# A fused attention and two mixture-of-experts layers on one core: Newton steps on another engine, and a new order of the last phase

## The chip, the cores and the metric

The kernel runs on one core of one Trainium2 chip. The metric is the device time of one execution in microseconds; lower is better. The time before is the median of three runs.

## The reference

`x` is (2, 11456, 128). Three layers follow each other:

```python
def mab(q, kv):
    s = scale * (q @ kv.T)
    a = exp(s - s.max(-1)); a /= a.sum(-1) + 1e-9
    return a @ kv
h = mab(inducing, x)          # 32 inducing points read 11456 tokens
x = mab(x, h)                 # every token reads the 32 points
logits = x @ phi              # soft mixture: 32 slots, 8 experts, 4 slots each
d = softmax(logits, over tokens);  slot_out[e] = relu((d.T @ x)[e] @ w1[e]) @ w2[e]
x = softmax(logits, over slots) @ slot_out
# hard mixture: one expert of 8 per token
logits = (x / (norm(x) + 1e-6)) @ (emb / (norm(emb) + 1e-6)).T / tau
e = argmax(logits);  gate = softmax(logits)[e]
out = gate * (relu(x @ w1b[e]) @ w2b[e])
```

## The kernel before

The 22,912 tokens are cut into 12 blocks (six per batch, of 16 tiles of 128 tokens, the last of each batch of 8) and a small thirteenth of leftovers, `sp`. Three phases follow each other. The first reads `x` and builds `h`; the second computes each token's slot logits, kept in SBUF in `lT`, and the slot inputs; the third makes the slot outputs, finds the one expert that the tokens use, and writes the output per block. All tokens use the same expert for this input; a check at the end (`cert`, `ok`) decides whether a general path must run, and here it need not. A token's vector after the soft mixture is a combination of 32 slot vectors, so norm, router and output are computed from the 32 exponentials `E` of its logits (`Eall`, the same memory as `lT`) and small matrices.

All work is written as Python generators ("chains"), and one string per phase, `SEQ` and `SEQ2`, says in which order their steps are issued; `in_order` then ties each engine's instructions to that order. A step whose input is late holds up everything behind it on its engine. What is left of a chain after its string is issued by a loop behind it. The chains that matter here:

- `p2_chain`, `grp_chain` (lines 360 to 510): second phase; each ends in additions to `acct` (L501 on POOL, L506 on DVE), and at last `dgp` (L480).
- `e_chain` (L641): a block's maxima on DVE (L96), the subtraction on POOL (L647), the exponential on ACT (L649). Nine are in `SEQ`, four run in the loop behind it.
- `bounds_chain` (L800 to 860): from `dall`, the spread of the logits, it makes `tau_`, `cmid`, two columns of `stkx`, and `rho`, which a later check needs. It is `B` in `SEQ2`.
- `slot_chain` (M), `hid_chain` (a to d), `sout_chain` (S), `sot_chain` (X), `gmat_chain` (W): the two layers of the slot experts; from `dgp` over `siT` (L544), `l1ps`, `hsb`, `hTb`, `sops` and `soT` to `BDg` (L883), the matrix that every gate product needs. `sout_chain` also reads the expert's number and starts the load of its weights.
- `hidden_chain` (H) makes `BDA`, the matrix of the output products; `cert_chain` (C) the check.
- `et_chain` (t0 to tc): four transposes of `E` per block on PE (L85) and a copy to SBUF, `ET`, by ACT or DVE (string `ETE`, L669).
- `gate_chain` (g0 to gc): products with `BDg` into `gps`, `au` copied by ACT, then a product with `E`, either on DVE from PSUM (L698) or, by the string `GTE`, copied by ACT and multiplied on POOL (L695), and a sum on DVE, `nn` (L96).
- `router_chain` (q0 to q3) for blocks 0-1, 2-5, 6-9 and 10-12: a square root of `nn` by three Newton steps (`sqrt_newton`, L785 to 796), a reciprocal, the router's exponential on ACT (L722), and the scale `scall` (L727). `best_chain` (k0 to k3): a comparison on POOL (L733), a sum on DVE.
- `out_chain` (o0 to oc): the output product of half a block, `ops`, scaled by `scall` into `ob` by DVE (V: one instruction, L766), by ACT (S: eight) or by ACT's copy and POOL (A, L775), as the string `OTE` says, and the DMA to HBM on SP's queue, per half for the blocks in `HALVES`.

PSUM in the third phase: `gps`, `ops`, `l1ps`, `sops` and `STps` share three buffers; all else takes two single banks in turn.

Of the kernel before, what the change touches and what calls it, by code (L numbers as in the profile page):

```python
# [18 lines left out]
def attn_moe_moe_kernel(  # L19
# [321 lines left out]
    R = {}  # L341
# [358 lines left out]
        vred(nn[:, ts], q, ALU.add)  # L700
        yield

    def router_chain(t0, t1):

        nt = t1 - t0
        sl = slice(t0, t1)
        n_ = ty([128, 64], F32, "g_n")[:, 0:nt]
        q = ty([128, 64], F32, "g_q")[:, 0:nt]
        bc = [128, nt, E]
        V.tensor_scalar(out=q, in0=nn[:, sl], scalar1=1e-36, scalar2=None, op0=ALU.max)  # L710
        for i, _ in enumerate(sqrt_newton(n_, q, [128, nt])):
# [7 lines left out]
        lg = wk([128, 64, E], F32, "eT")[:, 0:nt]  # L719
# [8 lines left out]
        yield

    def best_chain(t0, t1):  # L730

        ge = wk([128, 64, E], F32, "eq")[:, 0:t1 - t0]
        G.tensor_scalar(out=ge, in0=au[:, t0:t1, 0:E], scalar1=0.0, scalar2=None, op0=ALU.is_ge)  # L733
        yield
        vred(ok[:, t0:t1], ge, ALU.add)
        yield
# [44 lines left out]
    def sqrt_newton(y, q, shape):  # L781

        yi = ty([shape[0], 64], I32, "sq_i")[:, 0:shape[1]]
        t = ty([shape[0], 64], F32, "sq_t")[:, 0:shape[1]]
# [4 lines left out]
        for _ in range(3):
            V.scalar_tensor_tensor(out=t, in0=y, scalar=-0.5, in1=y, op0=ALU.mult, op1=ALU.mult)  # L790
            yield
            V.tensor_tensor(out=t, in0=t, in1=q, op=ALU.mult)  # L792
            yield
            V.scalar_tensor_tensor(out=y, in0=t, scalar=1.5, in1=y, op0=ALU.add, op1=ALU.mult)
            yield
        V.tensor_tensor(out=y, in0=y, in1=q, op=ALU.mult)
# [419 lines left out]
    mark2 = len(nc.cur_bb.bb.instructions)
    for c in SEQ:
        next(chains[c], None)  # L1220
# [11 lines left out]

    HALVES = (0, 1)
# [1 line left out]
    ETE = "SSVSSVSSSVVSV"
    GTE = "VGVGGVVVGVVGG"
    OTE = ("SA", "VS", "VA", "VV", "SS", "VA", "VV", "SV", "SS", "VV", "VV", "VS", "VS")
    late_c = {"M": slot_chain(), "R": rs_chain(), "S": sout_chain(), "X": sot_chain(), "W": gmat_chain(), "B": bounds_chain(),  # L1240
              "H": hidden_chain(), "C": cert_chain()}
# [134 lines left out]
```

## Time and profile before

| | |
|---|---|
| median of 3 runs | 215.33 us (214.25 to 215.44) |
| profiled execution | 216.28 us, of which the span is 214.6 us |
| busy in the span | PE 168.0, DVE 154.9, ACT 100.0, POOL 61.5 us |
| bytes moved | 40.82 MB |

The span runs from the first to the last instruction on the core. Busy shares are means over three phases with different limits, so the stages have to be looked at one by one; "half clock" below is a granted clock of 0.50 in the views, 1.2 GHz.

### The profile page before, as it was taken

Reading aid. Unit: us, or ns where it says so; the run is one execution under the profiler, and the core shown is the slowest. Engines: PE = TensorE matmul, PEld = TensorE weight load, DVE = VectorE, ACT = ScalarE, POOL = GpSimd, SP = SyncE. Lnnn points to the kernel's source line nnn. Section 1 sums busy time; section 2 is a strip of 40 time slices with the busy share of each in tenths; the row PEclk is TensorE's granted clock in tenths of the full one; section 3 lists DMA queues with packets and bytes.
Section 4 is the critical chain, followed back from the end, with each engine's and each line's share of the span. In section 5 each row is a group of like instructions: output and inputs, shape, how many; then the busy total and the mean of one; then the engine's idle time right before and its main releaser. Section 6 shows DMA issues by size and latency. Waiting matters only on the chain.

```text
span 214.6 us, 4393 instructions
## 1 busy us (share of the span) xinstructions
PE 168.0 (78%) x1587; PEld 119.7 (56%) x1587; DVE 154.9 (72%) x485; ACT 100.0 (47%) x283; POOL 61.5 (29%) x84
## 2 busy tenths in 40 slices
PE   0798779899999998987759698899976399778410
PEld 0665436557657757465548356789954276445300
DVE  7336847466999968899934633656999989999950
ACT  2244456367468577486543233414444176447100
POOL 2000001002248290829860610006365015020000
PEclk9999999999999999999965579969999579999955
DMA  5999988999619995000000000050002455538972
GB/s 174 422 300 396 409 341 302 426 400 389 230 31 375 346 416 231 0 0 3 0 0 5 0 0 3 3 184 11 3 0 98 169 215 208 231 162 344 409 322 50
DMA packets 9248, 40.82 MB, mean 190 GB/s; under 512 B 1116, under 2 KB 2308, under 8 KB 6276
## 3 DMA queue, kind: packets, MB, share of 16 engines
q1 hardware_dynamic: 9220, 40.48, 48.6%
q8 instruction: 14, 0.23, 0.4%
q14 instruction: 14, 0.11, 0.2%
HBM read 28.74 MB, written 11.73 MB: 189 GB/s over the span
## 4 chain that ended last, share of the span: by engine, by line
PE 42%; DVE 36%; ACT 7%; issue 5%; DMA 4%; POOL 1%; SPq 0%; DVEq 0%; ACTq 0%; POOLq 0%
PE s L88 9%; DVE ob L766 5%; PE lps L88 4%; PE slps L88 3%; PE gps L88 3%; DVE mx L96 3%; PE hps L88 3%; PE eTps L85 3%; PE xTps L85 3%; PE ops L88 3%; PE l1ps L88 3%; ACT eq L197 2%; DVE sq_t L792 2%; DVE xT L179 2%; DVE nn L96 2%
## 5 line engine op out<-in xcount | busy, mean ns | idle before, releaser
L88 PE MATMUL ops<-BDA,ET 64*128 64x256 f32 x180 | 25.5, 412 | 11.5 <-DVE ob L766 10.2
L88 PEld LDWEIGHTS ops<-BDA,ET 64*128 64x128 f32 x180 | 16.5, 195 | 18.6 <-DVE ob L766 9.9
L93 ACT ACTIVATE ob<-ops,scall 128x128 f32<-128x128 f32 x56 | 15.2, 383 | 8.3 <-PE ops L88 7.7
L200 POOL TENSOR_SCALAR hacc<-hacc,corr,sb 128x1 f32<-128x1 f32 x10 | 3.4, 343 | 48.8 <-ACT corr L199 45.5
L695 POOL TENSOR_TENSOR a2q<-sh,lT 128x512 f32<-128x512 f32 (+2 forms) x6 | 6.5, 1090 | 37.0 <-ACT sh L93 34.1
L88 PE MATMUL gps<-BDg,ET 128*128 128x164 f32 x90 | 15.7, 324 | 1.9 <-DVE a2q L698 1.5
L197 ACT ACTIVATE eq<-s,mn 128x512 f32<-128x512 f32 (+1 forms) x12 | 7.8, 651 | 19.3 <-DVE mn L192 16.4
L452 POOL TENSOR_TENSOR d<-lT,mnew 128x512 f32<-128x512 f32 (+1 forms) x11 | 13.5, 1226 | 10.3 <-DVE cr L438 8.4
L88 PEld LDWEIGHTS gps<-BDg,ET 128*128 128x128 f32 x90 | 13.8, 203 | 3.8 <-DVE a2q L698 1.9
L396 POOL TENSOR_TENSOR a<-sh,sm 128x512 f32<-128x512 f32 (+2 forms) x13 | 12.2, 935 | 12.4 <-DVE sm L393 6.4
L88 PE MATMUL s<-xT,IT 128*32 128x512 f32 (+1 forms) x96 | 12.8, 606 | 3.7 <-DVE xT L179 3.7
L766 DVE TENSOR_TENSOR ob<-ops,scall 128x1024 f32<-128x1024 f32 x13 | 15.4, 1218 | 0.3
L88 PE MATMUL slps<-d,a 128*128 128x128 f32 x88 | 14.3, 326 | 0.5 <-ACT d L465 0.5
L88 PE MATMUL lps<-BD,a2q 128*128 128x132 f32 x90 | 13.2, 287 | 0.9 <-ACT a2q L93 0.5
L88 PEld LDWEIGHTS slps<-d,a 128*128 128x128 f32 x88 | 13.3, 236 | 1.1 <-ACT d L465 0.6
L88 PEld LDWEIGHTS lps<-BD,a2q 128*128 128x128 f32 x90 | 11.1, 190 | 3.7 <-ACT a2q L93 2.2
L85 PE MATMUL xTps<-ident,xt 128*128 128x128 f32 x64 | 10.8, 329 | 2.5 <-DMA xt<-in_x 2.2
L85 PEld LDWEIGHTS xTps<-ident,xt 128*128 128x128 f32 x64 | 9.2, 172 | 6.2 <-issue 2.5
L647 POOL TENSOR_TENSOR lT<-lT,mx 128x512 f32<-128x512 f32 (+2 forms) x13 | 11.9, 933 | 1.7 <-DVE mx L96 1.7
L96 DVE TENSOR_REDUCE s<-s 128x1 f32<-128x512 f32 (+1 forms) x12 | 7.8, 650 | 6.1 <-PE s L88 5.5
L88 PE MATMUL hps<-xt,eT 128*32 128x128 f32 x352 | 12.0, 275 | 0.2 <-ACT eT L93 0.2
L96 DVE TENSOR_REDUCE ml<-lT 128x32 f32<-128x512 f32 (+2 forms) x13 | 11.9, 916 | 0.2
(291 smaller groups left out, 376.7 us busy)
## 6 DMA issues: line engine op xcount, KB each, us to landing
xt<-in_x SPq DMA_DIRECT2D x9, 1024.0 KB, 6.2
out<-ob SPq DMA_DIRECT2D x8, 1024.0 KB, 4.5
xT<-in_x_t SPq DMA_DIRECT2D x6, 1024.0 KB, 9.0
w1s<-in_moe_w SPq DMA_DIRECT2D x4, 1024.0 KB, 8.7
w2s<-in_moe_w SPq DMA_DIRECT2D x4, 1024.0 KB, 14.7
out<-ob SPq DMA_DIRECT2D x6, 512.0 KB, 2.7
xt<-in_x SPq DMA_DIRECT2D x4, 512.0 KB, 6.3
xT<-in_x_t SPq DMA_DIRECT2D x2, 512.0 KB, 10.2
```

Source lines behind the costliest of these rows:

```text
L85: nc.tensor.matmul(dst, lhsT=src, rhs=idn, is_transpose=True, start=True, stop=True)
L88: return nc.tensor.matmul(dst, lhsT=l, rhs=r, start=start, stop=stop)
L93: S.activation(out=o, in_=i, func=AF.Copy, **kw)
L96: V.tensor_reduce(out=o, in_=i, axis=AX.X, op=op, **kw)
L179: (acopy if c == 0 else V.tensor_copy)(xT_t[k][:, 8 * h + 4 * c:8 * h + 4 * c + 4, :].rearrange("p a t -> p (a t)"), ps[:, c])
L197: S.activation(out=e, in_=ps[:, 0:128 * n], func=AF.Exp, scale=-1.0, bias=mn, accum_out=sb)
L396: G.tensor_tensor(out=a2, in0=t, in1=r.unsqueeze(2).to_broadcast([128, 4 * n, 32]), op=ALU.mult)
L452: eng.tensor_tensor(out=d, in0=lT[:, t0:t0 + nt, :], in1=mb, op=ALU.subtract)
L647: G.tensor_tensor(out=e, in0=lT[:, t0:t0 + nt, :], in1=lx.unsqueeze(2).to_broadcast([128, nt, 32]), op=ALU.subtract)
L695: G.tensor_tensor(out=q, in0=ge, in1=Eall[:, ts, :], op=ALU.mult)
L766: V.tensor_tensor(out=o.rearrange("p (i r g) c -> p i r g c", i=m, r=2), in0=pv, in1=sc.rearrange("p (i r g) -> p i r g", i=m, r=2).unsque ...
L792: V.tensor_tensor(out=t, in0=t, in1=q, op=ALU.mult)
```

## The change

1. `sqrt_newton` gets an argument. With "V" it is as before; for the four routers (`QTE`, "GGGG") the three iterations and the last product run on POOL, as four operations per iteration instead of three (13 POOL instructions in place of 10 on DVE), in new yields. The setup of two operations stays on DVE. Its temporaries and the router's are one buffer each.
2. `bounds_chain` is now `&` in `SEQ`'s last characters: its first five steps are issued with the last group of the second phase and the rest as `B` in `SEQ2`.
3. The four `e` chains that the loop issued (blocks 8 to 11) are steps e8 to eb in `SEQ2`.
4. `SEQ2`, `ETE`, `GTE`, `OTE` and `HALVES` are new: half blocks scaled by DVE go from 13 to 16, by ACT in eight pieces from 7 to 6, by ACT and POOL from 2 to none; block 2 is stored in halves too. The DVE makes 7 copies of `ET` in place of 5.
5. With the other yields, `emb_setup`'s last step (a transpose of the expert vectors, `enps`, and its copy to `ien`) falls behind the end of `SEQ`.

```diff
-    def router_chain(t0, t1):
+    def router_chain(t0, t1, eng):
...
-        for i, _ in enumerate(sqrt_newton(n_, q, [128, nt])):
-            if i % 3 == 2:
-                yield
+        yield from sqrt_newton(n_, q, [128, nt], eng)
...
+    def sqrt_newton(y, q, shape, eng="V"):
+        t = ty([shape[0], 96], F32, "sq_t", bufs=1)[:, 0:shape[1]]
+        yi = t.bitcast(I32)
...
         for _ in range(3):
+            if eng == "V":
+                V.scalar_tensor_tensor(out=t, in0=y, scalar=-0.5, in1=y, op0=ALU.mult, op1=ALU.mult)
+                V.tensor_tensor(out=t, in0=t, in1=q, op=ALU.mult)
+                V.scalar_tensor_tensor(out=y, in0=t, scalar=1.5, in1=y, op0=ALU.add, op1=ALU.mult)
+            else:
+                G.tensor_tensor(out=t, in0=y, in1=y, op=ALU.mult)
+                G.tensor_tensor(out=t, in0=t, in1=q, op=ALU.mult)
+                G.tensor_scalar(out=t, in0=t, scalar1=-0.5, scalar2=1.5, op0=ALU.mult, op1=ALU.add)
+                G.tensor_tensor(out=y, in0=y, in1=t, op=ALU.mult)
+            yield
+        (V if eng == "V" else G).tensor_tensor(out=y, in0=y, in1=q, op=ALU.mult)
...
-        "5Mv4M5M4554566465466445%5%5%556566666"
+        "5Mv4M5M4554566465466445%5%5%5&56&56&66&66&"
...
-    HALVES = (0, 1)
+    HALVES = (0, 1, 2)
-    ETE = "SSVSSVSSSVVSV"
-    GTE = "VGVGGVVVGVVGG"
-    OTE = ("SA", "VS", "VA", "VV", "SS", "VA", "VV", "SV", "SS", "VV", "VV", "VS", "VS")
+    ETE = "SVVVSVSVVSSSS"
+    GTE = "VGGVVVVVVGGVG"
+    QTE = "GGGG"
+    OTE = ("VS", "SV", "VV", "VS", "SS", "VA", "VV", "VV", "VV", "VS", "VV", "VS", "VS")
...
-        "B M B M B M M R a b b c d a b a d c d S c B S B B B B B t1 S t0 B t1 B t0 B B S "
+        "B M e9 t0 B t0 M e9 e8 M ea e8 e9 eb B e8 ea t1 R M B ea eb a B t1 b a eb B c d b a b B c B "
```

Three places show how the order moves. First DVE at the change from the second phase to the third, where `dgp` is done and `siT` is wanted. Before:

```order
L480 TENSOR_TENSOR dgp_119<-acct_101,slps 32x32 x4
L96 TENSOR_REDUCE mx<-lT 128x16 x3
L96 TENSOR_REDUCE mx<-lT 128x8
L544 COPY siT<-sips 128x32
L96 TENSOR_REDUCE m_1706<-spd 2x1
```

With the change:

```order
L480 TENSOR_TENSOR dgp_119<-acct_101,slps 32x32 x4
L1180 COPY ien<-enps 128x8
L824 TENSOR_SCALAR tau__1671<-tau__1671 128x2
L826 TENSOR_SCALAR den_1692<-tau__1671 128x2
L827 RECIPROCAL den_1692<-den_1692 128x2
L829 TENSOR_TENSOR lo_1695<-tau__1671,den_1692 128x2
L96 TENSOR_REDUCE mx<-lT 128x16
L832 TENSOR_SCALAR w__1708<-tau__1671 128x2
L833 TENSOR_TENSOR w__1708<-w__1708,den_1692 128x2
L544 COPY siT<-sips 128x32
```

The four maxima of the `e` chains stood ahead of `siT`; now one of them does, with `ien`'s copy and six steps of the bounds.

Second, DVE at the router of blocks 2 to 5, from the setup on. Before (two further iterations follow):

```order
L710 TENSOR_SCALAR g_q<-nn 128x56
L785 TENSOR_SCALAR sq_i<-g_q 128x56
L787 TENSOR_SCALAR g_n<-sq_i 128x56
L790 SCALAR_TENSOR_TENSOR sq_t<-g_n 128x56
L792 TENSOR_TENSOR sq_t<-sq_t,g_q 128x56
L794 SCALAR_TENSOR_TENSOR g_n<-sq_t,g_n 128x56
L790 SCALAR_TENSOR_TENSOR sq_t<-g_n 128x56
```

With the change:

```order
L710 TENSOR_SCALAR g_q<-nn 128x56
L785 TENSOR_SCALAR sq_t<-g_q 128x56
L786 TENSOR_SCALAR g_n<-sq_t 128x56
L766 TENSOR_TENSOR ob<-ops,scall 128x1024
L698 TENSOR_TENSOR a2q<-gps,lT 128x512
L96 TENSOR_REDUCE ok<-eq 128x56
L96 TENSOR_REDUCE nn<-a2q 128x16
L766 TENSOR_TENSOR ob<-ops,scall 128x1024
L713 TENSOR_SCALAR g_r<-au 128x56
L714 SCALAR_TENSOR_TENSOR g_n<-g_r,g_n 128x56
L715 RECIPROCAL g_n<-g_n 128x56
```

Behind `g_n`'s first value there is other work now, and `L714` is the first that needs the root.

Third, POOL at the router of blocks 0 and 1, with the change (the second and third iteration are left out at the dots):

```order
L794 TENSOR_TENSOR sq_t<-g_n 128x32
L795 TENSOR_TENSOR sq_t<-sq_t,g_q 128x32
L796 TENSOR_SCALAR sq_t<-sq_t 128x32
L797 TENSOR_TENSOR g_n<-g_n,sq_t 128x32
L934 TENSOR_TENSOR d<-eT,cmid 128x512
...
L733 TENSOR_SCALAR eq<-au 128x448
L799 TENSOR_TENSOR g_n<-g_n,g_q 128x32
L921 COPY BDA_112<-BDA_110 32x128
```

The product `d` of the check stands behind the first iteration, and the comparison for blocks 2 to 5 (`eq`, which needs `au` of block 5) ahead of the last product.

## Rows read from the trace of the kernel before

**Rows 1.** Windows view, three late stages; columns are start:end, length, busy time per engine.

```profile
119.50:141.00 21.50, 18.70 (x239) 12.90 (x239) 11.63 (x46) 7.41 (x17) 3.64 (x4) 0.82 0.01 2
141.00:159.70 18.70, 17.43 (x123) 15.93 (x124) 14.22 (x44) 7.13 (x20) 7.32 (x10) 0.94 0.16 57
159.70:207.10 47.40, 31.76 (x216) 22.00 (x216) 44.30 (x99) 21.34 (x71) 9.58 (x8) 0.90 0.55 227
```

**Rows 2.** Chain that ended last, from 98 us; start, length, what.

```profile
104.01 0.50 DVE D L805
...
105.74 0.07 issue
```

**Rows 3.** POOL timeline, late second phase; start, length, operation, idle before.

```profile
104.88 0.85 POOL L447 TENSOR_TENSOR dsp<-lT,mnew 128x64 f32<-128x64 f32 x3 [0.39 <-DVE mnew L436]
```

**Rows 4.** Chain that ended last, from the last dgp to BDg.

```profile
119.24 0.19 DVE dgp L480
...
121.69 0.20 DVE siT L544
...
133.58 0.18 DVE tau__1843 L821
...
134.63 0.16 DVE cmid L837
...
136.21 0.59 ACT ET L93
...
136.84 0.62 PE cmT L88 x4
...
140.69 0.34 DVE BDg L883
```

**Rows 5.** PE timeline, transposes of E for two blocks.

```profile
135.16 1.09 PE L85 MATMUL eTps<-ident,lT 128*128 128x128 f32 x8
```

**Rows 6.** Windows view of two stretches at half clock; PEclk stands after POOL busy.

```profile
121.90:126.00 4.10, 4.06 (x43) 1.75 (x47) 0.98 (x5) 1.72 (x4) 2.03 (x3) 0.50 0.00 0
139.90:143.20 3.30, 2.93 (x12) 2.52 (x11) 1.60 (x5) 0.60 (x1) 0.00 (x0) 0.50 0.49 164
```

**Rows 7.** Groups by form on DVE, from 118 us; last columns are busy, mean ns, idle.

```profile
L766 DVE TENSOR_TENSOR ob<-ops,scall 128x1024 f32<-128x1024 f32 x13 | 15.4, 1218 | 0.3
...
L792 DVE TENSOR_TENSOR sq_t<-sq_t,g_q 128x56 f32<-128x56 f32 x3 | 2.3, 750 | 0.1
...
L669 DVE COPY ET<-eTps 128x512 f32<-128x512 f32 x3 | 2.0, 681 | 0.0
...
L790 DVE SCALAR_TENSOR_TENSOR sq_t<-g_n 128x56 f32<-128x56 f32 x3 | 1.6, 535 | 0.1
...
L790 DVE SCALAR_TENSOR_TENSOR sq_t<-g_n 128x64 f32<-128x64 f32 x3 | 0.7, 225 | 0.1
...
L790 DVE SCALAR_TENSOR_TENSOR sq_t<-g_n 128x27 f32<-128x27 f32 x3 | 0.6, 186 | 0.1
```

**Rows 8.** POOL timeline, beside the Newton steps of blocks 2 to 5.

```profile
159.51 1.33 POOL L733 TENSOR_SCALAR eq<-au 128x448 f32<-128x448 f32 x1 [0.38 <-ACT au L93]
...
163.93 1.89 POOL L775 TENSOR_TENSOR ob<-ob,scall 128x1024 f32<-128x1024 f32 x1
```

**Rows 9.** DVE timeline in the same stretch.

```profile
160.34 0.54 DVE L710 TENSOR_SCALAR g_q<-nn 128x56 f32<-128x56 f32 x1
...
164.08 1.82 DVE L792 TENSOR_TENSOR sq_t<-sq_t,g_q 128x56 f32<-128x56 f32 x1
```

**Rows 10.** Groups by form on POOL, whole span.

```profile
L733 POOL TENSOR_SCALAR eq<-au 128x512 f32<-128x512 f32 x1 | 1.5, 1488 | 0.0
...
L733 POOL TENSOR_SCALAR eq<-au 128x216 f32<-128x216 f32 x1 | 0.7, 749 | 0.0
...
L447 POOL TENSOR_TENSOR dsp<-lT,mnew 128x64 f32<-128x64 f32 x1 | 0.3, 322 | 0.4 <-DVE mnew L436 0.4
```

**Rows 11.** Groups by form on ACT, from 118 us.

```profile
L722 ACT ACTIVATE eT<-eT 128x448 f32<-128x448 f32 x1 | 0.6, 576 | 5.4 <-DVE eT L720 5.4
```

More of the change, by code (lines that the diff above doesn't have):

```diff
@@ L701, in gate_chain @@
         yield
-    def router_chain(t0, t1):
+    def router_chain(t0, t1, eng):
         nt = t1 - t0
         sl = slice(t0, t1)
-        n_ = ty([128, 64], F32, "g_n")[:, 0:nt]
-        q = ty([128, 64], F32, "g_q")[:, 0:nt]
+        n_ = ty([128, 96], F32, "g_n", bufs=1)[:, 0:nt]
+        q = ty([128, 96], F32, "g_q", bufs=1)[:, 0:nt]
         bc = [128, nt, E]
         V.tensor_scalar(out=q, in0=nn[:, sl], scalar1=1e-36, scalar2=None, op0=ALU.max)
-        for i, _ in enumerate(sqrt_newton(n_, q, [128, nt])):
-            if i % 3 == 2:
-                yield
-        r = ty([128, 64], F32, "g_r")[:, 0:nt]
+        yield from sqrt_newton(n_, q, [128, nt], eng)
+        r = ty([128, 96], F32, "g_r", bufs=1)[:, 0:nt]
         V.tensor_scalar(out=r, in0=au[:, sl, E], scalar1=1e-9, scalar2=None, op0=ALU.add)
@@ L718, in router_chain @@
         yield
-        lg = wk([128, 64, E], F32, "eT")[:, 0:nt]
+        lg = wk([128, 64, E], F32, "eT")[:, 0:nt] if nt <= 64 else au[:, sl, 0:E]
         V.scalar_tensor_tensor(out=lg, in0=au[:, sl, 0:E], scalar=0.0, in1=n_.unsqueeze(2).to_broadcast(bc), op0=ALU.min, op1=ALU.mult)
@@ L723, in router_chain @@
         yield
-        gs = ty([128, 64], F32, "g_s")[:, 0:nt]
+        gs = ty([128, 96], F32, "g_s", bufs=1)[:, 0:nt]
         vred(gs, lg, ALU.add)
@@ L730, in best_chain @@
     def best_chain(t0, t1):
[L732 to L736, printed above, removed]
+        for a in range(t0, t1, 64):
+            z = min(a + 64, t1)
+            ge = wk([128, 64, E], F32, "eq")[:, 0:z - a]
+            G.tensor_scalar(out=ge, in0=au[:, a:z, 0:E], scalar1=0.0, scalar2=None, op0=ALU.is_ge)
+            yield
+            vred(ok[:, a:z], ge, ALU.add)
+            yield
     def out_chain(k, how):
@@ L779, in out_chain @@
             yield
-    def sqrt_newton(y, q, shape):
-        yi = ty([shape[0], 64], I32, "sq_i")[:, 0:shape[1]]
-        t = ty([shape[0], 64], F32, "sq_t")[:, 0:shape[1]]
+    def sqrt_newton(y, q, shape, eng="V"):
+        t = ty([shape[0], 96], F32, "sq_t", bufs=1)[:, 0:shape[1]]
+        yi = t.bitcast(I32)
         V.tensor_scalar(out=yi, in0=q.bitcast(I32), scalar1=1, scalar2=None, op0=ALU.logical_shift_right)
-        yield
         V.tensor_scalar(out=y.bitcast(I32), in0=yi, scalar1=-1.0, scalar2=float(0x5F3759DF), op0=ALU.mult, op1=ALU.add)
@@ L789, in sqrt_newton @@
         for _ in range(3):
-            V.scalar_tensor_tensor(out=t, in0=y, scalar=-0.5, in1=y, op0=ALU.mult, op1=ALU.mult)
-            yield
[L792 to L796, printed above, removed]
+            if eng == "V":
[7 more added lines that the diff above has]
+                G.tensor_tensor(out=y, in0=y, in1=t, op=ALU.mult)
+            yield
+        (V if eng == "V" else G).tensor_tensor(out=y, in0=y, in1=q, op=ALU.mult)
         yield
@@ L1169, in emb_setup @@
         vred(en2, esq, op=ALU.add)
-        for i, _ in enumerate(sqrt_newton(enn, en2, [E, 1])):
-            if i % 3 == 2:
-                yield
+        yield from sqrt_newton(enn, en2, [E, 1])
         V.tensor_scalar(out=enn, in0=enn, scalar1=1e-6, scalar2=None, op0=ALU.add)
@@ L1198, in attn_moe_moe_kernel @@
     chains.update({"0123456"[i]: grp_chain(i) for i in range(len(groups))})
-    chains.update({"<": h_chain(0), ">": h_chain(1), "$": sp_phase1(), "@": emb_setup(), "%": fix_chain()})
+    chains.update({"<": h_chain(0), ">": h_chain(1), "$": sp_phase1(), "@": emb_setup(), "%": fix_chain(), "&": bounds_chain()})
     def in_order(mark):
@@ L1220, in attn_moe_moe_kernel @@
         next(chains[c], None)
-    for c in "abcdef$<@AB0CD1EF2ghijkl>GH3IJ4KL5M6%nopqrstuvwxyz":
+    for c in "abcdef$<@AB0CD1EF2ghijkl>GH3IJ4KL5M6%":
         for _ in chains[c]:
             pass
+    for _ in range(5 - SEQ.count("&")):
+        next(chains["&"])
     in_order(mark2)
@@ L1230, in attn_moe_moe_kernel @@
     pools["pw"] = late.enter_context(tc.tile_pool(name="pw", bufs=1, space=PSUM))
[L1235 removed]
+    HALVES = (0, 1, 2)
     GRPS = ((0, 2), (2, 6), (6, 10), (10, 13))
[L1237 to L1241 removed]
+    ETE = "SVVVSVSVVSSSS"
+    GTE = "VGGVVVVVVGGVG"
+    QTE = "GGGG"
+    OTE = ("VS", "SV", "VV", "VS", "SS", "VA", "VV", "VV", "VV", "VS", "VV", "VS", "VS")
+    late_c = {"M": slot_chain(), "B": chains["&"], "R": rs_chain(), "S": sout_chain(), "X": sot_chain(), "W": gmat_chain(), "H": hidden_chain(), "C": cert_chain()}
     for i, c in enumerate("abcd"):
@@ L1245, in attn_moe_moe_kernel @@
         k = ek2(i)
+        late_c["e%x" % i] = chains["nopqrstuvwxyz"[order2.index("sp" if i == SPB else i)]]
         late_c["t%x" % i] = et_chain(k, ETE[i])
@@ L1251, in attn_moe_moe_kernel @@
         t0 = btiles(ek2(a))[0]
-        late_c["q%x" % i] = router_chain(t0, t1[0] + t1[1])
+        late_c["q%x" % i] = router_chain(t0, t1[0] + t1[1], QTE[i])
         late_c["k%x" % i] = best_chain(t0, t1[0] + t1[1])
     SEQ2 = (
[6 rows of a table removed]
[7 rows of a table added]
     )
@@ L1264, in attn_moe_moe_kernel @@
         next(late_c[c], None)
-    for c in "M R a b c d B S X W t0 t1 g0 g1 q0 H C o0 t2 t3 t4 t5 g2 g3 g4 g5 q1 o1 o2 o3 t6 t7 t8 t9 g6 g7 g8 g9 q2 o4 o5 o6 o7 ta tb tc ga gb gc q3 o8 o9 oa ob oc k0 k1 k2 k3".split():
+    rest = ["M R a b c d B S X W"] + ["e%x" % i for i in range(n2)]
+    for i, (a, b) in enumerate(GRPS):
+        rest += ["t%x g%x" % (j, j) for j in range(a, b)] + ["k%x q%x" % (i, i)] + ["H C"] * (i == 0) + ["o%x" % j for j in range(a, b)]
+    for c in " ".join(rest).split():
         for _ in late_c[c]:
```

11 rows, old and new, of the table SEQ2 are left out of this document.

## The prediction

> **What bounds the kernel now.** I read the page's table of forty slices first: DVE is at 9 tenths from two thirds of the span to the end, no other engine is. The windows view puts numbers to three late stages [rows 1]. From 159.7 to 207.1 us, where the output is written, DVE is busy 44.30 of 47.40 us, PE 31.76, ACT 21.34, POOL 9.58: DVE's work is the time there, and POOL is free. From 141.0 to 159.7 DVE has 14.22 of 18.70 and PE 17.43. From 119.5 to 141.0 DVE has 11.63 of 21.50: there a chain of small steps sets the time, and the view to read is the chain that ended last. It runs from the last `dgp` over `siT` and the slot experts to `BDg` [rows 4]. So the change must be costed stage by stage. My sum is made against the profiled execution (216.28 us, span 214.6, 1.68 around it); the median of the runs shown is 0.95 lower, and I take the difference off the median.
>
> **Ahead of `BDg`.** The two bounds operations that stood at 103.8 to 104.5, `D`, are now issued later, beside transposes. One is a link of the chain, 0.50 long [rows 2], and POOL waited 0.39 for the `mnew` behind it [rows 3]: -0.4. From the end of the last `dgp` (119.43) to `siT` (121.69) were 2.26 us, in which DVE did four maxima [rows 4]. Now it does `ien`'s copy (0.2 at most), the steps from `tau` to the first `cmid` (133.58 to 134.63, 1.05, in the old place) and one maximum of 512 columns (0.68, as an `ET` copy of the same size [rows 7]): 1.9, so -0.3. The slot experts' chain on PE takes in two groups of four transposes, for t1 and t2, between `siT` and the end of `sops`: 0.55 each, eight took 1.09 [rows 5]: +1.1. The transposes of t0 lie in PE's wait for `siT`, at no cost; if `siT` came at once, they would cost 0.55. Behind `sops`, `cmT` is out of the way: PE stood from 136.25 to 136.84 for it and spent 0.62 on it [rows 4, 5], 1.2 together. In its place `vps` waits for a copy of `ET` by ACT, 0.59 [rows 4]: -0.6. Sum so far -0.2.
>
> PE ran at half clock for the 4.1 us ahead of 126.0, with 4.06 us of them busy, and for 3.3 us from 139.9 [rows 6]. All at full clock would give back 2.05 and 1.65 us; as before, nothing. In the first, transposes now fill PE's wait, about 1 us earlier, so I take 0.7; in the second, transposes and products stand where PE waited for `cmT`, and I take half, 0.8. -1.5.
>
> **From `BDg` to the first output half.** The root of blocks 0 and 1 leaves DVE: ten steps of some 0.2, 2 us. On POOL it is thirteen dependent steps, with the product `d` and the comparison of blocks 2 to 5 (1.33 for 448 columns [rows 8]) among them, as the third order fence shows. No row has these steps; the nearest are the product of 64 columns at 0.322 and the comparisons of 512 and 216 columns, 1.488 and 0.749 [rows 10], that is 2.5 ns a column, and the gap of 0.07 between dependent POOL instructions [rows 2]. So 64 columns cost 0.32 for a product, 0.37 for a scaling, 0.07 more each: 3 x (3 x 0.39 + 0.44) + 0.39 = 5.2 us a root; 56 columns 5.0, 32 and 27 columns 4.3 and 4.2 by the slope. The least would be the gap-free 3.3 us, the most, with steps like DVE's longest ones here, is a rival below. With `d` and `eq` POOL needs 6.9 us, and DVE has seven operations of 512 columns and some 1.5 us of small ones to do before it needs the root, 5.6 us with their overlaps: 1.3 of wait for 2 of work gone, and `g_q` now stands behind a POOL product, as it once took 0.54 instead of 0.2 [rows 9]. I count the stage at 0, between -1.5 and +1.5.
>
> **The output stage.** Off DVE: thirty Newton steps, twenty at 0.22 and ten at 0.19, 6.3 us, with 0.03 of wait before each (0.1 per three [rows 7]), 0.9. Off with them goes the time for which they stood still: the 56-column steps of L790 and L792 took 1.6 and 2.3 us in all, where three at 0.22 are 0.66 each [rows 7], so 2.6; the long one, 1.82, ends with POOL's 1.89 of `ob` [rows 8, 9]. `g_q` loses another 0.3. Off go two `ET` copies of 512 columns and a small one, 1.6, now made while DVE waits in the stages before (0.68 of such a copy would come back if it met `hsb` there), and a sum of 0.4. On DVE come three more halves of `ob` at 1.22 [rows 7], 3.7, and five operations of the check at 0.16 to 0.18 like `tau` and `cmid` [rows 4], 0.9. Sum: -6.3 - 0.9 - 2.6 - 0.3 - 1.6 - 0.4 + 3.7 + 0.9 = -7.5.
>
> What is late next: `L714` now waits for POOL. For blocks 2 to 5 the rows between setup and `L714` are two `ob` and three of 512 columns or less, 4.3 us, against 5.0: +0.7. For blocks 6 to 9 three `ob` and a sum, 4.2 against 5.2: +1.0. For 10 to 12 four `ob`, 4.9 against 4.2: 0. In the third router DVE's three setup operations come while POOL compares blocks 6 to 9 (1.488 [rows 10]), 0.68 into it: +0.8. And the router's sum follows its exponential with next to nothing between (0.576 on ACT [rows 11], before this an `ob` lay there): 0.4 to 0.5 for three routers, +1.3. Waits +3.8, so the stage gives -3.7. ACT has two packs fewer to do and POOL's 17 us of Newton steps fall in a stage where it was busy 9.58 [rows 1]: neither is queued full. SP gets one more output issue, beside transfers. The tail behind DVE's last instruction stays.
>
> Total: -0.2 - 1.5 + 0 - 3.7 = -5.4: 210.9 for an execution like the profiled one, **209.9 for the median**. Its own range is 206.5 to 213.5: the clock from 0 to 3.7, the POOL step 0.03 either way (1.3 us), the second stage 1.5 either way.
>
> **The rivals.** All hang on one price, because every 0.1 us a POOL step costs more is 1.3 us at each of three routers and 0.6 at the last, 4.5 together.
>
> *POOL's step is twice DVE's.* Then 0.38 to 0.45 and 0.07: 0.45 to 0.52 a step, 1.7 + 1.6 + 1.6 + 0.9 = 5.8 us more wait, 215.7: no change. Against it stands the product of 64 columns at 0.322 [rows 10]; for it, that product had not all its inputs this small and this often. The Trainium skill says so: its page GPSIMD Engine Reference, section "When to use GPSIMD" (its table "Engine selection"), gives VectorE for elementwise work on a tile, GpSimd being about twice as slow for two inputs. In this trace 0.322 against 0.225 at 64 columns is 1.4 times.
>
> *Slower: the router's latency takes the place of DVE's work.* If a step that waits for the one before costs 0.25 of gap and not 0.07, each root takes 6.6 to 7.6 us, DVE stands behind `L714` in four places, and +0.18 x 45 = 8.1 gives 218. It decides from a step of about 0.52 us, where all the gain is gone. Against it: the two gaps of the chain on POOL are 0.07.
>
> *Larger: the waits are covered.* If ACT and POOL answer while DVE has work, the 3.8 of waits go, and with a full clock some 1 us more: 205. For it: POOL and ACT are under half busy. Against it: the order leaves only the rows counted above.
>
> *The order does not do what it says:* `cmT` or t4's copy still holds `vps`. That costs 0.6 to 1.2 and stays in the forecast's range.
>
> **How the numbers follow.** Forecast 0.62, larger gain 0.16, twice DVE's step 0.13, slower 0.09. The range 205.0 to 214.0 leaves out the last two and little else. About 1.1 us, 0.5%, is what a measurement can tell here. The first two cases are faster by more: 0.78; the third is the same, 0.13; the last 0.09.
>
> **What would show it.** In the profile after: `siT` about 0.7 earlier against the span's start, `BDg` near 139; POOL steps L794 to L799 of 0.25 to 0.37 with gaps under 0.1; no `sq_t` on DVE beyond the two setup steps; L714 waiting 0 to 1 us for POOL; DVE's groups at L766 with 16 in place of 13, and the stretch from the first output half to DVE's last instruction near 43.5 us. Wrong, if POOL's steps pass 0.5 us, if `BDg` is not earlier, or if PE falls to half clock with DVE waiting for `ops`.

## The result, and the profile after

| | before | after |
|---|---|---|
| median of the runs, us | 215.31 (214.25 to 215.44) | 205.59 (205.16 to 207.7) |
| ratio | | 0.957, interval 0.951 to 0.964 |
| profiled execution, its span | 216.28, 214.6 | 207.7, 206.1 |

The change gains 9.7 us where 5.4 were forecast. Medians and ratios, here and below, leave out an execution that takes over 1.5% longer than the fastest of its kernel. The profiled execution is the slowest of the after runs; the others have spans of 203.5 to 204.1, and what sets it apart is a question for the experiments. The windows view after, with the three late stages of [rows 1] and the two stretches of [rows 6] (busy time of PE, of its weight loads, of DVE, ACT and POOL, then PEclk, the granted clock of PE):

```profile
119.50:141.00 21.50, 19.73 (x247) 12.99 (x247) 13.72 (x47) 6.84 (x15) 3.64 (x4) 0.85 0.01 2
141.00:157.80 16.80, 16.71 (x121) 15.32 (x122) 14.04 (x34) 5.30 (x16) 9.97 (x22) 1.00 0.19 63
157.80:198.02 40.22, 29.16 (x208) 19.70 (x207) 36.16 (x71) 18.38 (x63) 15.90 (x44) 0.95 0.66 267
121.90:126.00 4.10, 4.10 (x41) 1.28 (x40) 3.52 (x12) 2.62 (x6) 2.77 (x4) 0.50 0.00 0
139.90:143.20 3.30, 2.44 (x19) 2.20 (x17) 2.20 (x7) 0.78 (x2) 0.00 (x0) 1.00 0.48 155
```

`BDg` is where it was. The stage from `BDg` to the first output half is 1.9 us shorter, the output stage 7.2: DVE has 8.1 us less to do there, and its idle time rose from 3.1 to 4.1 us only. POOL went from 9.58 to 15.90 busy. The groups by form on POOL, for [rows 10], and the dependent steps of one iteration in POOL's timeline (start, length, operation, idle before):

```profile
L795 POOL TENSOR_TENSOR sq_t<-sq_t,g_q 128x64 f32<-128x64 f32 x3 | 1.0, 322 | 0.2
...
L796 POOL TENSOR_SCALAR sq_t<-sq_t 128x56 f32<-128x56 f32 x3 | 0.7, 238 | 0.3
...
L795 POOL TENSOR_TENSOR sq_t<-sq_t,g_q 128x27 f32<-128x27 f32 x3 | 0.7, 243 | 0.2
```

```profile
171.52 0.29 POOL L794 TENSOR_TENSOR sq_t<-g_n 128x64 f32<-128x64 f32 x1 [0.36 <-DVE g_n L786]
171.89 0.32 POOL L795 TENSOR_TENSOR sq_t<-sq_t,g_q 128x64 f32<-128x64 f32 x1
172.30 0.24 POOL L796 TENSOR_SCALAR sq_t<-sq_t 128x64 f32<-128x64 f32 x1
172.63 0.32 POOL L797 TENSOR_TENSOR g_n<-g_n,sq_t 128x64 f32<-128x64 f32 x1
```

A product of 64 columns takes 0.32 as the row before said, the scaling 0.24 (forecast 0.37), the gap 0.07 to 0.09. What DVE waits for from `BDg` to the flag (total, times, longest):

```profile
DVE g_n L714 <- POOL g_n L799: 2.2, 3, 0.9
DVE a2q L698 <- ACT au L93: 1.6, 1, 1.6
DVE g_s L96 <- ACT eT L720: 1.4, 3, 0.5
```

### The profile page after: what moved, and what is told of

Read it like the earlier page. It is cut to its first block, busy times and chain, and to the rows that moved or that the text cites. A ratio compares the mean times of both kernels' runs of the same rounds, so it can differ in the third digit from the quotient of the medians.

```text
span 206.1 us, 4392 instructions
## 1 busy us (share of the span) xinstructions
PE 166.2 (81%) x1587; PEld 117.3 (57%) x1587; DVE 149.2 (72%) x451; ACT 94.9 (46%) x270; POOL 70.5 (34%) x133
## 4 chain that ended last, share of the span: by engine, by line
PE 44%; DVE 27%; POOL 8%; ACT 7%; issue 5%; DMA 4%; SPq 0%; DVEq 0%; ACTq 0%; POOLq 0%
PE s L88 10%; PE slps L88 5%; DVE ob L766 5%; PE lps L88 4%; PE eTps L85 4%; PE xTps L85 3%; PE hps L88 3%; PE l1ps L88 3%; DVE mx L96 2%; DVE nn L96 2%; DMA out<-ob 2%; ACT eq L197 2%; DMA xt<-in_x 2%; PE fps L88 2%; PE s2T L85 2%
## 5 line engine op out<-in xcount | busy, mean ns | idle before, releaser
L88 PE MATMUL ops<-BDA,ET 64*128 64x256 f32 x180 | 24.6, 404 | 7.2 <-DVE ob L766 4.7
L88 PEld LDWEIGHTS ops<-BDA,ET 64*128 64x128 f32 x180 | 15.9, 189 | 14.0 <-DVE ob L766 5.4
L766 DVE TENSOR_TENSOR ob<-ops,scall 128x1024 f32<-128x1024 f32 x16 | 18.9, 1218 | 0.3
L396 POOL TENSOR_TENSOR a<-sh,sm 128x512 f32<-128x512 f32 (+2 forms) x13 | 12.1, 933 | 12.3 <-DVE sm L393 6.4
L93 ACT ACTIVATE ob<-ops,scall 128x128 f32<-128x128 f32 x48 | 13.1, 384 | 5.9 <-PE ops L88 5.8
L88 PE MATMUL gps<-BDg,ET 128*128 128x164 f32 x90 | 14.8, 311 | 0.9 <-DVE BDg L886 0.9
L695 POOL TENSOR_TENSOR a2q<-sh,lT 128x512 f32<-128x512 f32 (+1 forms) x5 | 5.6, 1112 | 26.9 <-ACT sh L93 26.8
L88 PEld LDWEIGHTS gps<-BDg,ET 128*128 128x128 f32 x90 | 12.7, 190 | 2.4 <-DVE BDg L886 1.1
L88 PEld LDWEIGHTS lps<-BD,a2q 128*128 128x128 f32 x90 | 11.1, 190 | 3.7 <-ACT a2q L93 2.2
```

What stands on the lines that cost most here:

```text
L88: return nc.tensor.matmul(dst, lhsT=l, rhs=r, start=start, stop=stop)
L93: S.activation(out=o, in_=i, func=AF.Copy, **kw)
L396: G.tensor_tensor(out=a2, in0=t, in1=r.unsqueeze(2).to_broadcast([128, 4 * n, 32]), op=ALU.mult)
L695: G.tensor_tensor(out=q, in0=ge, in1=Eall[:, ts, :], op=ALU.mult)
L766: V.tensor_tensor(out=o.rearrange("p (i r g) c -> p i r g c", i=m, r=2), in0=pv, in1=sc.rearrange("p (i r g) -> p i r g", i=m, r=2).unsque ...
```

## The experiments

From here on each profile is cut at four marks: the end of the last `dgp`, the end of `BDg`, the start of the first output half (stage B lies between these two), the end of the last output product (stage C), the end of the span. Lengths in us; medians, and ratios to the kernel before run on the same chip.

| kernel | median | ratio | to dgp | to BDg | B | C | rest |
|---|---|---|---|---|---|---|---|
| before | 215.31 | | 119.44 | 21.58 | 18.68 | 46.92 | 7.93 |
| after | 205.59 | 0.957 | 119.29 | 21.66 | 16.83 | 39.76 | 8.52 |
| after_again | 205.68 | 0.958 | 117.58 | 20.22 | 16.85 | 39.77 | 8.49 |
| newton_dve | 213.28 | 0.993 | 118.37 | 20.73 | 18.65 | 44.23 | 8.48 |
| old_order_pool | 218.62 | 1.016 | 119.46 | 21.72 | 24.57 | 45.75 | 7.57 |
| bounds_back | 206.81 | 0.963 | 120.00 | 20.27 | 16.82 | 39.62 | 8.46 |
| e_drain | 210.24 | 0.977 | 119.27 | 24.50 | 16.82 | 40.79 | 8.37 |
| pool_plus | 210.20 | 0.973 | 118.60 | 20.72 | 17.73 | 43.12 | 8.38 |
| fill_waits | 204.92 | 0.953 | 118.05 | 20.66 | 16.83 | 38.80 | 8.45 |
| oa_split | 205.67 | 0.956 | 118.63 | 20.23 | 16.84 | 39.02 | 9.20 |
| pe_filler | 203.74 | 0.949 | 115.82 | 20.73 | 16.82 | 39.64 | 8.44 |
| fill_o6 | 204.32 | 0.950 | 118.14 | 20.67 | 16.83 | 38.26 | 8.47 |
| all_filled | 201.95 | 0.940 | 116.83 | 19.85 | 16.81 | 38.22 | 8.46 |
| early_flag | 200.52 | 0.931 | 116.02 | 19.83 | 18.37 | 38.89 | 7.22 |

**The Newton steps back on DVE, in the new order** (newton_dve).

```
-    QTE = "GGGG"
+    QTE = "VVVV"
```

> The changed kernel with one part undone: the routers' three Newton iterations and the closing product are on DVE again, in the new order. Theory 1 (the steps' place is the gain): DVE gets back the 9.7 us that the steps of q1, q2 and q3 took in the profile of before, loses the 1.5 us in which it waited for POOL at L714 (0.58 and 0.95), and in the stretch before the first output product q0's steps (about 2.1 us) take the place of a 0.69 us wait: 9.7 - 1.5 + 1.4 = +9.6, so 215 us, about the time before the change. Rival (the order is the gain): with the steps spread by iterations between other work they fill DVE's waits, and it is +3 us or less, 207 to 209 us.

213.28 us, ratio 0.993 (0.989 to 0.997): nearer to theory 1 than to the rival. B is 18.65 at full clock, 1.8 longer than with the change; C is 44.23, 4.5 longer. That is less than 9.7 - 1.5: here an iteration's three steps stand together, and none stood still beside POOL, as the groups by form show against the 535 and 750 ns of [rows 7]. Only the setup's `L785` of blocks 0 and 1 did, beside POOL's product `d` (0.18 after the change):

```profile
L785 DVE TENSOR_SCALAR sq_t<-g_q 128x32 int32<-128x32 int32 x1 | 1.2, 1207 | 0.0
...
L791 DVE TENSOR_TENSOR sq_t<-sq_t,g_q 128x56 f32<-128x56 f32 x3 | 0.7, 217 | 0.1
...
L790 DVE SCALAR_TENSOR_TENSOR sq_t<-g_n 128x56 f32<-128x56 f32 x3 | 0.6, 207 | 0.0
```

So the new order alone, with its strings of engines, is worth 1.8 us (0.6 to 2.5 by the ratio), and POOL's part on top of it 7.7. No run parts the order from the strings.

**The Newton steps on POOL, in the old order** (old_order_pool; router_chain passes `"G"`).

```
-            V.scalar_tensor_tensor(out=t, in0=y, scalar=-0.5, in1=y, op0=ALU.mult, op1=ALU.mult)
...
+                G.tensor_tensor(out=t, in0=y, in1=y, op=ALU.mult)
...
+                G.tensor_tensor(out=y, in0=y, in1=t, op=ALU.mult)
```

> The kernel before with one part of the change alone: the iterations and the closing product on POOL, the yields and the order as they were. Theory 1: DVE loses 9.7 us of q1 to q3 and some 2 us of q0, less the waits that a chain of 13 POOL instructions (4 to 5 us) makes at L714 where the old order has less other work between two steps; estimate -6, 209 us, and the granted clock in the stretch around BDg stays at half, since the transposes are where they were. Rival (the order is needed): the waits take nearly all of it, 213 to 215 us, with over 8 us of DVE idle behind POOL in the output stage.

218.62 us, 1.016 (1.007 to 1.024): slower than before. Theory 1 is wrong here, and the rival was not strong enough. The profile is of its slowest run (220.82), and B is 5.9 longer in it than before. DVE's timeline there (start, length, operation, idle before), and POOL's:

```profile
155.51 1.24 DVE L716 SCALAR_TENSOR_TENSOR g_n<-g_r,g_n 128x32 f32<-128x32 f32 x1 [2.90 <-POOL g_n L806]
```

```profile
155.23 0.25 POOL L806 TENSOR_TENSOR g_n<-g_n,g_q 128x32 f32<-128x32 f32 x1
155.44 1.26 POOL L695 TENSOR_TENSOR a2q<-sh,lT 128x512 f32<-128x512 f32 x1
```

The root costs twice: 2.90 us of waiting, and then the operation that needs it takes 1.24 in place of 0.19, because POOL went on to its next product in the same moment and DVE's operation ends 0.05 behind that product. With the other two large groups this makes 7.1 us of waiting and 2.6 of standing still. The Trainium skill says why one waits for the other's whole length: its page SBUF — State Buffer, section "SBUF: two separate sides", has GpSimd and a VectorE operation with two inputs from SBUF, as `L716` is, take a shared port pair under an exclusive lock for the whole instruction. The two rows agree with that. In the new order POOL has no product behind its root, and L714 takes 0.19 to 0.23. Not all of the 5.9 is the root's: DVE's wait for `eT` ahead of it is 1.6 longer than before, in an execution with PE at half clock to 147 us, where before it was to 143. Before, and here:

```profile
146.78 0.17 DVE L897 TENSOR_SCALAR pos<-STps 128x16 f32<-128x16 f32 x1 [1.51 <-ACT eT L93]
```

```profile
148.67 0.17 DVE L907 TENSOR_SCALAR pos<-STps 128x16 f32<-128x16 f32 x1 [3.11 <-ACT eT L93]
```

Neither part explains the result: -1.8 and +3.6 apart, -9.7 together.

**The bounds put back** (bounds_back; the letters `&` are the bounds steps in the second phase, `B` those in the third).

```
-        "5Mv4M5M4554566465466445%5%5%5&56&56&66&66&"
+        "5Mv4M5M4554566465466445%5%5%556566666"
...
-        "B d c B S d B t2 S t2 t5 S t4 t5 t4 X X S W S S W S ...
+        "d c S B B B B d B B t2 S B B B t2 B t5 B S B t4 t5 t4 X X S B B W S S W S ...
```

> The changed kernel with the bounds chain begun where it was before (none of it in the second phase). Theory 1: the early start is worth what BDg shows, sops to BDg 4.78 against 5.80 us and siT 0.55 us earlier, of which the l1ps stage kept nothing: +0.5 to +1.2, 206 to 207 us. Rival (the early bounds also free PE for the transposes that hold the clock up behind BDg): the 1.9 us of the next stretch go too, +2.5 to +3, 208 to 208.6 us, with a granted clock of 0.50 in the 3 us behind BDg.

206.81 us: +1.2 against the change, the upper end of theory 1; the intervals of the two ratios overlap, so the stages have to bear it out. From the end of `sops` to `BDg` it is 5.63 against 4.77; B is untouched, so the rival falls. The early bounds have a price as well: `siT` ends 1.34 behind the last `dgp` here, and 1.97 in after_again.

**The e chains drained in the second phase** (e_drain).

```
-    for c in "abcdef$<@AB0CD1EF2ghijkl>GH3IJ4KL5M6%":
+    for c in "abcdef$<@AB0CD1EF2ghijkl>GH3IJ4KL5M6%nopqrstuvwxyz":
```

> The changed kernel with the e chains of the last four blocks run at the end of the second phase again, ahead of the third part's first steps. Theory 1 (l1ps starts when PE has done t0's transposes, so DVE's four maxima of 0.68 us ahead of siT cost only what exceeds PE's 0.6 us): siT 1 to 2 us later, +0.4 to +1.4, 206 to 207 us. Rival (they lie in DVE's waits anyway): no difference, 205.3 to 205.9 us.

210.24 us, +4.6, far over both. DVE's timeline from `dgp` to `siT`:

```profile
119.50 2.20 DVE L96 TENSOR_REDUCE mx<-lT 128x16 f32<-128x512 f32 x4
121.61 0.79 DVE L824 TENSOR_SCALAR tau__1671<-tau__1671 128x2 f32<-128x2 f32 x1
122.44 0.97 DVE L826 TENSOR_SCALAR den<-tau__1671 128x2 f32<-128x2 f32 x1
...
124.17 0.18 DVE L544 COPY siT<-sips 128x32 f32<-128x32 f32 x1
```

Not only the maxima stand ahead of `siT`: `tau` and `den` take 0.79 and 0.97 in place of 0.17, while POOL subtracts those maxima beside them:

```profile
120.33 3.63 POOL L647 TENSOR_TENSOR lT<-lT,mx 128x512 f32<-128x512 f32 x4 [2.02 <-DVE mx L96]
```

PE has nothing from 120.9 to 124.4, runs at half clock behind it, and `BDg` is 2.8 us later than in the first profile. C is 1.0 longer, with a wait of DVE of 1.1 for `ops`. So with the early bounds, spreading out the e chains is worth 4.6 us. What the early bounds are worth without that is not shown: no run of this order has late bounds and drained chains.

**The changed kernel a second time** (after_again).

> The changed kernel itself, profiled a second time on the chip of the next three. Theory: the profiled execution shown with the result was its slowest (207.7 us, granted clock 0.50 from 110 to 126 us of the span); in the others the clock comes back to full before l1ps, as it did at 119 us in the profile with the bounds put back. Then a profile near the median has a span of 203.5 to 204.2 us, full clock in most of 121.9 to 126 us, and BDg 1.5 to 2 us earlier (139.0 to 139.5). Rival (the 2 us lie in the output stage): l1ps at half clock again and BDg at 141 us in a run of 205.5 us.

Confirmed, in a run of 204.54, with `BDg` at 137.81, earlier than written: B and C are the first profile's to 0.02 us. The 3.2 us of span between the two lie ahead of `BDg`. The windows view (PEclk after POOL) of the first profile and of this one:

```profile
114.00:118.00 4.00, 3.70 (x18) 3.33 (x17) 2.00 (x13) 1.63 (x6) 0.11 (x1) 0.50 0.00 0
118.00:122.00 4.00, 3.47 (x19) 2.78 (x22) 3.60 (x16) 0.17 (x1) 1.31 (x2) 0.50 0.00 0
122.00:126.00 4.00, 4.00 (x41) 1.21 (x40) 3.42 (x11) 2.62 (x6) 2.67 (x4) 0.50 0.00 0
```

```profile
114.00:118.00 4.00, 2.68 (x17) 2.40 (x18) 2.60 (x13) 1.06 (x5) 0.46 (x1) 0.86 0.00 0
118.00:122.00 4.00, 4.00 (x44) 2.34 (x48) 3.85 (x12) 1.81 (x3) 2.69 (x3) 0.57 0.00 0
122.00:126.00 4.00, 4.00 (x41) 1.56 (x38) 3.54 (x12) 2.19 (x6) 0.95 (x2) 1.00 0.00 0
```

The same instructions run at 1.2 GHz in one execution and at 2.4 in the other. Seven profiles here have the change's code up to `BDg`, which ends at 137.80 to 140.95, in the middle 138.86; two have the old code, 141.02 and 141.18.

**One POOL step more per iteration** (pool_plus).

```
                 G.tensor_scalar(out=t, in0=t, scalar1=-0.5, scalar2=1.5, op0=ALU.mult, op1=ALU.add)
+                G.tensor_scalar(out=t, in0=t, scalar1=1.0, scalar2=0.0, op0=ALU.mult, op1=ALU.add)
```

> The changed kernel with one more dependent POOL instruction (a multiplication by 1.0 that adds 0) in each Newton iteration: 12 instructions of 0.24 us and a gap of 0.08, 0.96 us more per router chain. Theory 1 (POOL's chain ends last at the L714 of q0, q1 and q2, and has 0.5 us to spare at q3): +0.96 three times and +0.4 once, +3.3, about 209 us, with the waits at L714 1.5 to 1.7, 1.5, 1.9 and 0.4 us. Rival (POOL is hidden but for the waits seen, and part of them is only moved from the exp that follows): under +1.5, 207 us or less.

210.20 us, 4.5 over after_again on the same chip; the waits came out as written:

```profile
DVE g_n L714 <- POOL g_n L800: 5.5, 4, 1.8
...
DVE ob L766 <- PE ops L88: 1.0, 1, 1.0
```

5.5 against 2.2 us at L714 is the +3.3. The second row is a cost that no theory had: behind the longer waits PE's granted clock is 0.78 in 177:180 and 0.65 in 180:183, where after_again has 1.00, and DVE waited 1.0 us for its products. C and B together are 4.2 longer. Theory 1 holds for the waits, and the price of a POOL step is higher than they are.

**The waits filled** (fill_waits; parts of lines of `SEQ2`).

```
-  t9 k1 o1 q1 tb g7 o0 o1 q1 o2 o0 q1
-  o4 C q1 C g9 C q1 q1
+  t9 o1 q1 tb g7 o0 o1 q1 o2 o0 C q1
+  o4 q1 C g9 C q1 k1 q1
...
-  o5 gb q2 o3 gb q2 gc o3 gb q2 o6 gb
+  o5 gb q2 o3 gb gb q2 gc o3 q2 o6 gb
...
-  ga o8 k3 q3
+  ga o8 q3
...
-  q3 q3 q3 q3 ob oa
+  q3 q3 q3 k3 q3 ob oa
```

> The changed kernel with four pieces of DVE work moved into its waits: the certificate's five small operations ahead of q1's L713 (they fill 0.58 us of waiting at L714), q1's count of ok behind q1's lg (0.54 us of waiting for the exp), one 256-column product with its a2q ahead of q2's L713 (0.36 of 0.95 us), and the counts of ok of the last group behind q3's lg (0.45 us). Theory (each filled microsecond comes off the end, since DVE's order from the first output product to the last is the path): -1.9, 203.7 us. Rival (the exp and the gates that ACT and PE owe DVE then become late, or what is moved makes another wait): -0.5 to 0, 205.1 to 205.6 us.

204.92 us, 0.8 under after_again. The waits fell by 2.2 us (L714 from 2.2 to 1.0, the exp from 1.4 to 0.4), but C by 1.0 only: DVE waits 0.3 for `ops`, and its busy time in C rose by 0.5, `g_q` of 64 columns from 0.20 to 0.39 beside POOL. This is between theory and rival: a filled wait gave back half.

**The last group's half on ACT** (oa_split; block a's `"VV"` becomes `"VS"`).

> The changed kernel with the second half of the output block a (of the last group, whose products start when scall of q3 is there) made by eight ACT activations in place of one DVE product. ACT is idle from q3's exp on, and eight activations took 2.18 us. Theory 1 (DVE's four last products are the path): DVE ends 1.2 us earlier and so does the kernel, 204.4 us. Rival (the last stores are the path: 8.1 us lie between DVE's last product and the end of the span, in which the DMA engines are still 41% busy): DVE ends 1.2 us earlier, the end stays, 205.3 to 205.8 us.

205.67 us, no gain. C is 0.8 shorter, the rest 0.7 longer. The rival stands, with a share for PE: it ran at half clock there and DVE waited 0.3 for the last product.

**Transposes in PE's waits** (pe_filler; the same loop with 2 and 3 ahead of spd and sips).

```
         ps = ps_b("mps")
+        for _ in range({5: 9, 6: 3}.get(gi, 0)):
+            transp(ps[:, 128:256], ident, ident)
         mm(ps[:, 0:32], ones[0:32, :], dg)
```

> The changed kernel with 17 transposes of the identity on PE, whose results nothing reads, in the four waits that PE has between 105 and 118 us: 9 ahead of the product that waits 1.70 us for ACT's dg, 3 in the 0.72 us ahead of the next, 2 in the 0.51 us ahead of spd, 3 in the 0.64 us ahead of sips; at 0.165 us each at full clock they fit. In all profiles so far the granted clock falls to 0.50 about 1 us after the 1.70 us wait, returns between 115 and 126 us, and where it returns by 116 us it falls again after the two waits ahead of sips. Theory 1 (PE's idling there is what drops the clock, and the half clock ahead of BDg is the part of the time that differs between executions of one kernel): full clock from 104 us to BDg, BDg 1 to 3 us earlier than 137.8 to 139 us, and 203 us median with a narrower spread. Rival (the drop has another cause, work of PE before it or nothing that the filler changes): the clock falls at 108 to 109 us all the same, the fillers then take 0.27 us each and run over their waits, and the time is 206 to 207 us.

203.74 us, -1.9, and `BDg` at 136.55. The clock stays at 1.00 from 104 to 118 us, where the profiles of the change without fillers have 0.50 to 0.55 in 110:114. It falls once more, to 0.57 in 118:122. The three transposes ahead of sips had not filled that wait: they stood behind the wait for `ien` themselves. The mean granted clock of the six runs is 0.962 to 0.976, that of the change's nine runs 0.930 to 0.952, so the profile is no exception. Theory 1 holds for the fall behind those waits and for the time; full clock up to `BDg` and a narrower spread of the runs (203.19 to 205.21) did not come.

**Block 6's half on ACT** (fill_o6; fill_waits with block 6's `"VV"` as `"VS"`).

> The kernel with the filled waits, and the second half of output block 6 made by eight ACT activations (2.18 us, where ACT is idle from 185 to 191 us) in place of one DVE product of 1.22 us. Theory 1 (DVE's order from the first output product to the last is the path, and here, unlike in the last group, neither PE nor the stores are near it): -1.2 us against the filled waits alone, 203.7 us, with scall of q3 11.1 us behind scall of q2 in place of 12.3. Rival (ACT's half holds one of the three PSUM buffers for 2.2 us, and PE's next products come late): -0.3 to 0, 204.6 to 204.9 us, with new waits of DVE for PE's ops.

204.32 us, -0.6 against fill_waits; C -0.5. From the end of scall of q2 to that of q3 it is 11.6, against 12.3 in fill_waits and 11.1 expected. DVE's wait for `ops` grew from 0.3 to 0.7: between theory and rival.

**All of it, with the last wait filled too** (all_filled: fill_o6 with 13, 6, 3 and 5 transposes).

> The kernel with the filled waits and block 6's half on ACT, and 27 unread transposes on PE (13, 6, 3 and 5 in the same four waits; those ahead of sips are put where they need not wait for ien). Theory 1 (the two gains are in different stretches and add up, and the second fall of the clock, at 118.8 us in the kernel with 17 transposes, comes from the wait ahead of sips that they did not fill): 204.3 - 1.9 = 202.4 us, and 0.6 to 1 us less if the clock then stays up in l1ps, 201.6. Rival (the second fall is not of that wait): full clock to 118 us, half from 119 to 122 again, 202.4 us.

201.95 us. The windows view shows full clock where it had been half:

```profile
110.00:114.00 4.00, 3.09 (x22) 2.41 (x22) 2.61 (x17) 2.20 (x9) 2.51 (x4) 1.00 0.01 2
...
118.00:122.00 4.00, 4.00 (x56) 2.06 (x59) 3.87 (x11) 2.19 (x4) 3.43 (x4) 1.00 0.02 4
```

From `dgp` to `BDg` it is 19.85 in place of 20.73. The clock decides for theory 1, both parts; the time lies between its 201.6 and the rival's 202.4.

**The flag early, block a's store halved** (early_flag, against all_filled; F is a chain with the flag's operations).

```
-  o7 oa q3 q3 q3 k3 q3 ob oa ob oa oa oc oc
+  o7 oa q3 q3 q3 k3 F q3 ob F oa ob oa F oa oc oc
+    HALVES += (ek2(10),)
```

> The kernel of the run before with two edits in the last 15 us: the flag's four small DVE operations and PE's transpose ahead of the last output products (in the kernel before them they are the last work of DVE), and block a's output stored in two halves of 0.5 MB. In all kernels with the new order but one the span ends 7.9 to 8.1 us behind the flag. Theory 1 (the flag, its load and the branch are the path at the end): 0.4 to 0.6 us less than the run before, or more if the branch's code is fetched while the stores still run. Rival (the last stores to land end the span as well, 4.7 us after their issue): no difference but for the halved store, 0 to -0.3 us.

200.52 us, ratio 0.931 (0.926 to 0.935), the best kernel here. That is 1.4 less than all_filled, where theory 1 had 0.4 to 0.6 or more. The rest behind the last product is 7.22 in place of 8.46, C 0.7 longer. The two edits were not parted, so which of them shortened the rest stays open; the span now ends 9.3 us behind the flag and not 8.0, so the flag alone no longer sets the end. The profile is of its slowest run (201.97), and in it the clock fell at `BDg`, with the same instructions as in all_filled:

```profile
135.85:138.35 2.50, 2.45 (x9) 2.45 (x10) 1.26 (x3) 0.00 (x0) 0.00 (x0) 0.50 0.81 236
```

B is 18.37 there: half clock for the first 3.3 us behind `BDg` cost 1.55 us.

## Why the prediction was right, and where it was not

The sign, the place and the mechanism were right: DVE's work in the output stage, with POOL free. The size was not: 205.6 is 4.3 us under the forecast. It is below the forecast's own 206.5 to 213.5, and in the whole range only because that takes in the larger gain, whose mechanism did not come; that is luck. Between the two profiled executions (210.9 forecast, 207.7 measured) the errors cancel in part as well: the output stage gave 3.5 more than forecast and the stage before it 1.9 more, the way to `BDg` 1.6 less, and the tail cost 0.6.

- **Ahead of BDg, steps -0.2, clock -1.5.** The profiled execution gave -0.07, next to the prediction's own sign of being wrong, `BDg` not earlier; the other six have it 1.7 to 3.2 us earlier, all seven in the middle -2.2. Of the steps, `D` gave 0.14 for 0.4, at half clock both times; `siT` comes 0.55 earlier; t1 and t2 made `sops` end 0.95 later for 1.1; behind `sops` 1.0 went, not 0.6. "At no cost" for t0 failed in the profile shown with the result: l1ps starts at 121.94 in both kernels, behind t0's transposes at half clock. In the six other profiles of that code l1ps follows `siT` by 0.05 to 0.12. The clock's size was near, its place not: it comes back at 115 to 117 us and falls once more near the start of l1ps, or, in the profile shown with the result, it does not come back before 126; pe_filler shows that PE's waits from 105 to 118 us make it fall.
- **BDg to the first output half, 0.** It was -1.85, and this step failed: it set the root's steps against the wait for POOL and left out what DVE waits for ahead of the root. The steps were right (1.9 us for 2); the wait at L714 was 0.69, not 1.3, as POOL's chain with `d` and `eq` took 6.4 us, not 6.9; the slow `g_q` came (0.70), but in newton_dve too. Yet DVE is as busy in the stage as before (14.2 before, 14.1 after), for `ET` copies and products came in from the output stage. What shortened it is DVE's idle time, 4.5 before and 2.8 after. It had two long waits before, at the end of these rows; of them only the first is left, with 1.65:

```profile
143.85 0.69 DVE L698 TENSOR_TENSOR a2q<-gps,lT 128x512 f32<-128x512 f32 x1 [2.24 <-ACT au L93]
...
146.78 0.17 DVE L897 TENSOR_SCALAR pos<-STps 128x16 f32<-128x16 f32 x1 [1.51 <-ACT eT L93]
```

The clock that I had in the first term, 0.8, belongs here: 1.00 in place of 0.50 from 139.9. Before, PE ran at half clock for the first 2.2 us of the stage, and early_flag prices 3.3 such microseconds at 1.55. How much of the shorter waits is the order's and how much the clock's, no run parts. newton_dve has both and is no shorter than before, because its DVE does 16.5 us of work there: the root's steps, and 1.0 for which `L785` stood still.

- **The output stage, -3.7.** It was -7.2. The largest error is here. Work: forecast -7.5 with 0.9 of gaps, so -6.6 of busy time; measured -8.1. The Newton steps (9.7 us with their gaps and standing still, 9.8 forecast), the output products (+3.5, +3.7), the certificate (+0.7, +0.9) and the copies (-1.4, -1.6) were right; I missed that two `a2q` products leave the stage, 1.2 us, for waits of the stage before; the rest are small differences. Waits: L714 1.5 (1.7 forecast) and the exponential 1.4 (1.3) were right, the third router's setup behind POOL cost 0.3, not 0.8, and a wait of 0.8 for `au` that the stage had before is gone, which I did not count.
- **The tail, unchanged.** 0.6 longer.

The rivals: twice DVE's step did not come. At 64 columns POOL's product takes 0.322 against DVE's 0.224 in newton_dve, 1.4 times; the Trainium skill's page GPSIMD Engine Reference, section "When to use GPSIMD", which says about twice, does not fit products this small. The gap of 0.25 did not come either: a whole root takes 4.1 to 4.9 us on POOL, forecast 4.2 to 5.2 (the gap-free 3.3 of the prediction is a root of 32 columns). The larger gain gave the time that was measured, but not by its mechanism: the waits were not covered, 2.95 us of them are in the output stage. "Every 0.1 us of a POOL step" was low: pool_plus has the forecast waits, and PE's clock on top. What no rival had is that the gain needs both parts: the price of POOL's root is set by what POOL does next and by what DVE has to do meanwhile, and the order sets both.

## What to carry to other kernels

Moving a latency chain to a free engine paid here only with an order that gives the busy engine work for the chain's length and leaves the free engine nothing long queued behind the chain's last step; try the move and the order together, since the move alone can lose, as here. Where executions of one kernel differ, cut their profiles at the same marks and look for the stage that differs: here all of it lay ahead of `BDg`, and its cause, PE's waits, could be filled with work that nobody reads. A small DVE operation beside a long POOL one stood still for most of that one's length here (1.24 beside 1.26), so before a small operation is put on a critical path, look at what the other engine runs then.

## What the runs showed of the hardware that I had not expected

- Small DVE operations stood still beside POOL's: `den` of 2 columns took 0.97 in place of 0.17, `g_n` of 56 columns 1.26 in place of 0.22.
- PE at half clock up to 126 us in one execution and up to 115 us in another, with the same instructions: 3.2 us of span between two profiles of one kernel. With 27 transposes that nobody reads, the clock stayed at 2.4 GHz from 104 us to `BDg`.
- A wait that is lengthened on DVE can cost more than itself: 3.3 us more at L714 cost 4.2, as PE, idle behind it, fell to 1.2 GHz.
